# Pack output projection in 256-column strips, summed on VectorE instead of GpSimd

## The chip, the cores and the metric

One core of a Trainium2 chip runs the whole program. The metric is device time in microseconds (us) of one launch, the median over runs. TensorE (PE, with weight loads as PEld), VectorE (DVE), ScalarE (ACT), GpSimd (POOL) and SyncE (SP, which issues DMAs) each work through a queue of their own; semaphores order them against each other.

## What is computed

```python
for s in range(64):                       # 64 segments, 32 tokens each
    h = concat([mem, x_s])                # 8 memory rows + 32 tokens, 512 wide
    q, k, v = h @ Wq, h @ Wk, h @ Wv      # 32 heads of 128
    p = softmax(mask(q @ k.T * scale))    # (40 x 40 per head)
    o = (p @ v) @ Wo                      # back to 512 wide
    mem = o[:8]; out_s = o[8:]            # memory goes to the next segment
h = x + A(layernorm(x))
out = h + gelu(layernorm(h) @ w1 + b1) @ w2 + b2
```

The memory rows of one segment are the input of the next, so the 64 segments run one after another; the MLP at the end runs over all 2,048 tokens.

## The kernel before

The first 689 us are the 64 segments, some 10.3 us each; the rest is the MLP. All weights stay in SBUF. Four segments make a block (128 tokens, tile `tb`). In each segment 32 rows are handled directly: the 8 memory rows and the first 24 tokens of the segment. The last 8 tokens of each of a block's four segments do not depend on memory in their q, k and v, so they are collected into a **pack** of 32 rows, and the packs' projections are done for a whole block at a time: K of a pack in a block's first segment, Q in the second, V in the third, and the output projection of the previous block's pack (`wo_B`, L1211) in the fourth. These pieces stand in the tables `ORDERS` as F0 and F1, and they fill TensorE while the segment's own chain is elsewhere.

The chain of a segment, in the names that the profile prints: memory and tokens `hT`; projections into `ps` (L873, and L606 where weights are kept); copies `kq` on ScalarE (L891, L892); transposes `QT` and `KALL` on VectorE (L914); scores (L1042); softmax on VectorE and ScalarE (`nmc`, `EC`, `rsc`, `PC`, `PTC`); p @ v (L1080, L1085) into `quad`; copies `OT`; output projection `wo` (L1176); transpose `TT` (L1188); and two sums (L1182) that write the memory rows of the next segment's `hT`. The scores among the 24 tokens run beside it: L1110, then `nma`, `SA`, `sma`, `rsa` on VectorE, `PA` on GpSimd (L1131), `PTA`, four copies `BD` (L1137), p @ v at L1148, one segment later.

TensorE's array is used as four column groups of 32 columns. In `wo` (`wo_units`, L1166) a pair of groups takes each half of the heads and each group of a pair takes 256 output columns, so two partial sums have to be added. In `wo_B` of this kernel each group takes a quarter of the heads and all 512 output columns; the result is transposed as a whole (`TTB`, L1219), and 14 GpSimd instructions fold the four partial sums into `opT` (L1228 to L1232). `fold` hands them out over the tails of the following segments, 3, 5 and 6 at a time. Then `nat` (L1244) transposes the block's `opT` by DMA into `oN`, adds it to `xr` (L1249), takes LayerNorm statistics (L1254, L1258; GpSimd L1259, L1260) and stores the rows.

The order on ScalarE, VectorE and GpSimd is found by a scheduler when the program is built: it goes through the operations by planned times (`PLAN`, in us from the start of the segment; kinds that are not in the table go by rank) and puts each into the first gap of its engine's line that is long enough by the durations noted in the code. TensorE's order is written out in `ORDERS`. `align` (L478) gives each segment a fixed place in TensorE's blocks of 256 instructions (`PHASE`): where a segment would start elsewhere, it puts extra weight loads (L871, at most 8 in a unit of four matmuls, the same weights again) in front of its matmuls until the place is right. `wire` (L420) decides which dependences become semaphore waits.

Of the kernel before, what the change touches and what calls it, by code (L numbers as in the profile page):

```python
# [96 lines left out]
        "KB1": (12.13, None, None, None),  # L97
        "QTB1": (None, 8.75, None, None),
        "VSB1": (None, None, 10.85, None),
        "TTB": (None, None, None, 10.96)}  # L100
HOME = {'OTB': 'act', ('SC0', 0): 'act', 'ZCm0': 'pool', 'kq1': 'act', 'SP1': 'act', 'VS1': 'act', 'VSl1': 'act', 'OTm0': 'act', 'SAp': 'dve', 'PA': 'pool', 'VSB1': 'act'}
STEP = 10.28
OPEN_BANK = dict(K0=4, K1=5, Q0=6, Q1=7, V0=5, V1=4, SC0=6, SC1=7, SA=5, WO=4)
# [15 lines left out]


class Op:
    __slots__ = ("eng", "fn", "reads", "writes", "idx", "gidx", "deps", "sig", "sigcount", "waits",
                 "tag", "pad", "held", "name", "is_dma", "dma_sem", "dur", "mode", "rank", "start", "succ", "prev", "ni", "at", "dma_count", "alts", "kind", "span")

    def __init__(self, eng, fn, reads, writes, name, dur, mode):
# [15 lines left out]
class Sched:  # L141
    def __init__(self, nc, self_sync=("act", "dve", "pool")):
        self.nc = nc
        self.rec = []
        self.last_writer = {}
        self.readers = {}
        self.self_sync = set(self_sync)
        self.pe_order = []
        self.buckets = {}
        self.tag = None  # L150
        self.dmas, self.soft = [], []

    def op(self, eng, fn, reads=(), writes=(), dur=0.2, mode=0, name=None, after=(), ni=8):
        o = Op(eng, fn, tuple(reads), tuple(writes), name, dur, mode)
        o.ni = ni
        o.tag = self.tag
        o.gidx = len(self.rec)
        deps = set()
        for k in o.reads:
            excl = isinstance(k, tuple) and k[0] == "ps"  # L160
            w = self.last_writer.get(k)
            if w is not None:
                deps.add(w)
            if excl:
                deps.update(self.readers.get(k, ()))
        for k in o.writes:
            w = self.last_writer.get(k)
            if w is not None:
                deps.add(w)
            deps.update(self.readers.get(k, ()))  # L170
        deps.update(a for a in after if a is not None)
        deps.discard(o)
        o.deps = sorted(deps, key=lambda d: d.gidx)
        for k in o.reads:
            if isinstance(k, tuple) and k[0] == "ps":
                self.last_writer[k] = o
                self.readers[k] = []
            else:
                self.readers.setdefault(k, []).append(o)
        for k in o.writes:  # L180
            self.last_writer[k] = o
            self.readers[k] = []
        self.rec.append(o)
        if eng == "pe":
            if self.tag is None:
                self.pe_order.append(o)
            else:
                self.buckets.setdefault(self.tag, []).append(o)
        return o
# [230 lines left out]
    def wire(self):  # L420
# [9 lines left out]
        for o in self.all_ops:  # L430
            E = o.eng
            cand, dwaits = {}, []
            for p in o.deps:
                if p.is_dma:
                    if p not in dma_known[E]:
                        dwaits.append(p)
                    continue
                if p.eng == E and E not in self.self_sync:
                    continue
                if p.idx > cand.get(p.eng, -1):  # L440
                    cand[p.eng] = p.idx
            waits = []
            for F, i in cand.items():
                if know[E][F] >= i:
                    continue
                p = self.streams[F][i]
                p.sig = True
                waits.append(p)
            for p in waits:
                for g in engs:  # L450
                    know[E][g] = max(know[E][g], snap[p][g])
                know[E][p.eng] = max(know[E][p.eng], p.idx)
                dma_known[E] |= dsnap[p]
            for p in dwaits:
                if p in dma_known[E]:
                    continue
                waits.append(p)
                dma_known[E].add(p)
                for g in engs:
                    know[E][g] = max(know[E][g], snap[p][g])  # L460
                dma_known[E] |= dsnap[p]
            o.waits = sorted(waits, key=lambda p: -(p.start + p.dur + self.lat(p, o))) if SORT else waits
            s = dict(know[E])
            if not o.is_dma:
                s[E] = o.idx
            snap[o] = s
            ds = set(dma_known[E])
            if o.is_dma:
                ds.add(o)
            dsnap[o] = ds  # L470
# [90 lines left out]
P = 128  # L561
# [62 lines left out]
def build_kernel(nc, A_x, A_mem0, A_Wq, A_Wk, A_Wv, A_Wo, B_w1, B_b1, B_w2, B_b2, out):  # L624
# [3 lines left out]
    with st:  # L628
        def sb(name, shape, dt=BF16):
            return st.enter_context(nc.sbuf_tensor(name, shape, dt))  # L630
# [44 lines left out]
        OT = sb("OT", [P, 2, H, 32])  # L675
        OTB = sb("OTB", [P, 2, H, 32])
        TT = sb("TT", [P, 2, DC, 2, 32], F32)
        TTB = sb("TTB", [P, DC, 4, 32], F32)
        TTS = sb("TTS", [64, 2, 4, 32], F32)
        opT = sb("opT", [P, 2, DC, P])  # L680
        stt = sb("stt", [P, 2, 6], F32)
        agg = sb("agg", [P, 2, 2], F32)
# [475 lines left out]
        def slot(h):  # L1158
            j = (h % 16) // 4
            return 16 * (j // 2) + 8 * (h // 16) + 4 * (j % 2) + h % 4  # L1160
# [48 lines left out]
                    rows()  # L1209

        def wo_B(bk, bank):  # L1211
            for q in range(8):
                def f(e, q=q):
                    for j in range(4):
                        ins = e.matmul(ps[bank][32 * j:32 * j + 32, :], OTB[:, bk % 2, slot(8 * j + q), :], WO[:, 8 * j + q, :], start=(q == 0), stop=(q == 7),  # L1215
                                       tile_position=(0, 32 * j), skip_group_check=True)
                    return ins
                S.op("pe", f, reads=[("WO", g, a) for g in range(8) for a in range(2)] + [("OTB", bk % 2, sg) for sg in range(4)], writes=[("ps", bank)], dur=0.2135, mode=MC, ni=8)
            S.op("dve", lambda e: e.transpose(TTB[:].rearrange("p c q t -> p (c q t)"), ps[bank][:, :]), reads=[("ps", bank)], writes=["TTB"], dur=t_dve(512) + 0.02)  # L1219
            o = opT[:, bk % 2, :, :].rearrange("p c (s t) -> p c s t", s=4)[:, :, :, NA:SEG]  # L1220

            def chunk(c):
                t = TTB[:, c:c + 2]

                def sums(q):
                    def f(e):
                        x, y = [v[0:32, :, q].rearrange("p c (s t) -> p c s t", s=4) for v in (t, TTS)]
                        return e.tensor_tensor(o[32 * q:32 * q + 32, c:c + 2], x, y, ALU.add)  # L1228
                    return lambda after: S.op("pool", f, reads=["TTB", "TTS"], writes=[("opB", bk % 2)], dur=0.31, after=after)
                return [lambda after: S.op("pool", lambda e: e.tensor_copy(TTS[0:64], t[64:128]), reads=["TTB"], writes=["TTS"], dur=0.4, after=after),  # L1230
                        lambda after: S.op("pool", lambda e: e.tensor_tensor(t[0:64], t[0:64], TTS[0:64], ALU.add), reads=["TTB", "TTS"], writes=["TTB"], dur=0.73, after=after),
                        lambda after: S.op("pool", lambda e: e.tensor_copy(TTS[0:32], t[32:64]), reads=["TTB"], writes=["TTS"], dur=0.41, after=after)] + [sums(q) for q in range(4)]  # L1232
            folds.extend(chunk(0) + chunk(2))

        folds = []

        def fold(n, after=()):
            tag, S.tag = S.tag, None
            for f in folds[:n]:
                S.narrow(f(after))  # L1240
            del folds[:n]
            S.tag = tag

        def nat(bk):  # L1244

# [149 lines left out]
        for s in range(NS):  # L1395
# [46 lines left out]
            def tail(s):  # L1442
                S.tag = (s, "SAT")
                sa_tail(s)
                n = 14 if s == NS - 1 else (3, 5, 6, 0)[s % 4] if s // 4 < NTB - 3 else (7, 7, 0, 0)[s % 4]
                moved = []
                for f in late[::-1]:
                    moved.append(f([S.last_writer[("PTC", 1)]] + [o_ for o_ in moved if o_]))
                late[:] = now
                now.clear()  # L1450
                behind = [S.last_writer[(k, 1)] for k in ("PC", "PCa")] + [o_ for o_ in moved if o_]
                if folds:
                    fold(n, behind + [S.last_writer[("BD", s % 2, j)] for j in range(4 * (s == NS - 1))])
                if turned and s % 4 == 3:
                    for f in turned:
                        f(behind)
# [139 lines left out]
        for i in range(2):  # L1596
            f = slice(i * (F // 2), (i + 1) * (F // 2))
            for c in range(DC):
# [5 lines left out]
        busy = (BANK["FB"], BANK["WO"])  # L1604
        free = [b for b in range(4, 8) if b not in busy]
        early, later = (free + sorted(set(busy)))[:2], (free + sorted(set(busy)))[2:]
        rest = {0: lambda: wo(NS, later[-1], mem=False), 2: lambda: nat(NTB - 2), 4: lambda: pv_a(NS - 1), 5: lambda: pv_a_ev(NS - 1), 7: lambda: (wo_B(NTB - 1, later[-1]), fold(14)),
                9: lambda: wo(NS + 1, later[0], mem=False), 11: lambda: nat(NTB - 1)}
        rest = dict(zip((0, 1, 3, 4, 6, 7, 9), rest.values()))
        for n, fc in enumerate(range(3, FC)):  # L1610
# [84 lines left out]
```

## Time and profile before

| | us |
|---|---|
| median of 3 runs (804.85 to 806.24) | 805.77 |
| span of the profiled execution | 804.0 |
| PE busy | 772.7 |
| DVE busy | 616.6 |
| ACT busy | 543.0 |
| POOL busy | 350.7 |
| granted TensorE clock, mean | 0.996 |

The device time of the profiled execution is not listed apart; its span is 1.8 us under the median of the runs, and what lies around the span is taken as that. Busy shares cover the whole span: a matmul's end is modelled, so a busy PE says only that matmuls were in its pipe. What the segments wait for is read from the timeline: a row gives start, length in us, engine, line, operation, out<-in, shape and count, and in brackets how long the engine was idle before it and for whom.

### The profile page before, as it was taken

The page shows a single profiled execution, that of the slowest core. Times are in us where ns is not written, and L with a number is a line of the kernel's source. Part 1 is how long each engine was busy: PE and PEld are TensorE (multiplying, and loading weights), DVE is VectorE, ACT ScalarE, POOL GpSimd, SP SyncE. Part 2 cuts the span into 40 slices and gives each one's busy share as a digit, 9 for nine tenths or more (in the row PEclk, how much of TensorE's full clock was granted, in tenths as well). Part 3 has the DMA queues.
Part 4 walks back from the last instruction along what each step waited for, and adds up shares of the span by engine and source line. Part 5 has one row for each costly group of instructions (what it writes and reads, how often), then busy time and mean ns, then how long its engine had stood idle before and what let it go on. Part 6 is the DMA issues. An engine that isn't in the chain of part 4 may idle for free.

```text
span 804.0 us, 43669 instructions
## 1 busy us (share of the span) xinstructions
PE 772.7 (96%) x19317; PEld 419.3 (52%) x18821; DVE 616.6 (77%) x1975; ACT 543.0 (68%) x1618; POOL 350.7 (44%) x886
## 2 busy tenths in 40 slices
PE   3788999999999999999999999999999999999998
PEld 1345555555555555555555555555555555544443
DVE  3267898898989898998989898989898887824211
ACT  2456777777777777777777787777777777743342
POOL 5023334545454545454545454545463535367200
PEclk9999999999999999999999999999999999999999
DMA  9960010110101010101010102020212131264200
GB/s 338 393 188 16 4 30 11 27 34 23 37 18 42 18 43 14 46 10 47 8 50 10 49 11 51 10 51 3 51 29 63 37 87 32 89 167 132 69 27 26
DMA packets 65450, 48.04 MB, mean 60 GB/s; under 512 B 29028, under 2 KB 61676, under 8 KB 65260
## 3 DMA queue, kind: packets, MB, share of 16 engines
q1 hardware_dynamic: 64928, 44.98, 18.9%
q8 instruction: 150, 2.46, 1.3%
q14 instruction: 40, 0.33, 0.1%
q10 hardware_dynamic: 332, 0.27, 0.1%
HBM read 31.08 MB, written 8.13 MB: 49 GB/s over the span
## 4 chain that ended last, share of the span: by engine, by line
PE 91%; DVE 3%; DMA 2%; SPq 2%; ACT 1%; issue 0%
PE ps L873 43%; PE ps L1176 16%; PE ps L606 7%; PE quad L1584 6%; PE ps L1577 5%; PE ps L1215 4%; PE quad L1080 3%; DMA WQ<-in_A_Wq_dram 2%; SPq L776 2%; PE ps L1110 2%; PE quad L1042 2%; PE ps L1370 2%; PE quad L1148 1%; PE quad L1085 1%; DVE PC L1067 1%; ACT kq L891 1%
## 5 line engine op out<-in xcount | busy, mean ns | idle before, releaser
L873 PE MATMUL ps<-WQ,hT 128*32 128x512 bf16 x2048 | 157.0, 382 | 3.5 <-DVE hT L1182 3.3
L1176 PE MATMUL ps<-WO,OT 128*32 128x256 bf16 x4224 | 141.5, 275 | 1.0 <-ACT OT L891 1.0
L873 PE MATMUL ps<-WV,hT 128*32 128x512 bf16 x1780 | 138.1, 379 | 0.0
L892 ACT ACTIVATE kq<-ps 128x512 bf16<-128x512 f32 x146 | 87.2, 597 | 57.5 <-PE ps L873 57.2
L1131 POOL TENSOR_TENSOR PA<-SA,rsa 128x256 bf16<-128x256 f32 x64 | 39.8, 622 | 181.4 <-DVE rsa L1124 169.6
L891 ACT CAST kq<-ps 128x512 bf16<-128x512 f32 x160 | 93.3, 583 | 29.8 <-PE ps L873 29.8
L1176 PEld LDWEIGHTS ps<-WO,OT 128*32 128x32 bf16 x4224 | 96.2, 96 | 23.6 <-ACT OT L891 4.0
L1137 POOL COPY BD<-PTA 32x192 bf16<-32x192 bf16 x256 | 95.7, 374 | 16.5 <-DVE PTA L1133 0.8
L1067 DVE SCALAR_TENSOR_TENSOR PC<-EC,rsc,even 128x128 bf16<-128x128 f32 x256 | 94.5, 370 | 6.7
L873 PE MATMUL ps<-WK,hT 128*32 128x512 bf16 x1292 | 92.3, 379 | 0.0
L873 PEld LDWEIGHTS ps<-WQ,hT 128*32 128x32 bf16 x2048 | 56.4, 96 | 63.7 <-issue 19.3
L914 DVE STREAM_TRANSPOSE KALL<-kq 128x256 f32<-128x256 f32 x160 | 70.5, 441 | 21.3 <-ACT kq L891 19.0
L891 ACT CAST VS<-ps 128x512 bf16<-128x512 f32 x189 | 83.9, 444 | 0.9
L1059 ACT ACTIVATE EC<-quad,nmc 128x64 f32<-128x64 f32 x252 | 76.8, 310 | 5.7
L606 PE MATMUL ps<-WK,hT 128*32 128x512 bf16 x756 | 74.3, 379 | 0.0
L891 ACT CAST OT<-quad 128x128 bf16<-128x128 f32 (+1 forms) x208 | 68.4, 352 | 4.9 <-PE quad L1085 0.7
L914 DVE STREAM_TRANSPOSE QT<-kq 128x256 f32<-128x256 f32 x128 | 57.0, 446 | 16.1 <-ACT kq L892 15.0
L873 PEld LDWEIGHTS ps<-WV,hT 128*32 128x32 bf16 x1780 | 49.4, 96 | 34.9 <-issue 1.0
L1580 ACT ACTIVATE WQ<-ps,b1t 128x512 bf16<-128x512 f32 x42 | 28.9, 687 | 52.0 <-PE ps L1577 52.0
L1122 ACT ACTIVATE SA<-SA 128x256 f32<-128x256 f32 x64 | 26.7, 417 | 52.2 <-DVE SA L1121 48.8
L873 PEld LDWEIGHTS ps<-WK,hT 128*32 128x32 bf16 x1292 | 35.9, 97 | 46.6 <-issue 20.2
L1228 POOL TENSOR_TENSOR opT<-TTB,TTS 32x64 bf16<-32x64 f32 x128 | 40.3, 315 | 31.7 <-DVE opT L1182 22.5
(159 smaller groups left out, 1475.9 us busy)
## 6 DMA issues: line engine op xcount, KB each, us to landing
WV<-in_A_Wv_dram SPq DMA_DIRECT2D x4, 1024.0 KB, 10.4
WK<-in_A_Wk_dram SPq DMA_DIRECT2D x4, 1024.0 KB, 18.1
WQ<-in_A_Wq_dram SPq DMA_DIRECT2D x4, 1024.0 KB, 19.4
WO<-in_A_Wo_dram SPq DMA_DIRECT2D x16, 256.0 KB, 7.7
v_last<-VSB SPq DMA_DIRECT2D x60, 64.0 KB, 3.1
VBD<-v_last SPq DMA_DIRECT2D x60, 64.0 KB, 2.9
h_mid<-xr SPq DMA_DIRECT2D x16, 128.0 KB, 1.8
WQ<-h_mid SPq DMA_DIRECT2D x4, 512.0 KB, 4.4
```

The source lines that it names most:

```text
L606: return e.add_instruction(mybir.InstMatmult(name="I-%d" % (4000000 + _kept[0]), engine=mybir.EngineType.PE, start_tensor_calc=start, stop ...
L873: ins = e.matmul(o, l, m, start=(k == 0), stop=(k == DC - 1), tile_position=(0, 32 * j), skip_group_check=True)
L891: return {"act": (lambda e: e.copy(out, src), t_act(n, ps_)), "dve": (lambda e: e.tensor_copy(out, src), 0.155 + 1.0e-3 * n * fast)}
L892: return {"act": (lambda e: e.mul(out, src, scale_), t_act(n, ps_)), "dve": (lambda e: e.tensor_scalar(out, src, scale_, None, ALU.mult), ...
L914: S.op("dve", lambda e: e.transpose(out, src), reads=[("kq", i)], writes=[key], dur=t_dve(256) + 0.02)
L1059: return e.activation(EC[:, r, sl, :], o[:, sl, :], ACTF.Exp, bias=nmc[:, r, sl:sl + 1], accum_out=smc[:, r, sl:sl + 1])
L1067: S.op("dve", lambda e, sl=sl, xc=xc: e.scalar_tensor_tensor(PC[:, r, :, :, sl], xc, rsc[:, r, sl:sl + 1], ev, ALU.mult, ALU.mult), reads= ...
L1137: S.narrow(S.op("pool", lambda e, j=j, rows=rows: e.tensor_copy(BD[rows, par, :, j, :, :], PTA[rows, :, 0:NA, :]), reads=["PTA"], writes=[ ...
L1176: ins = e.matmul(ps[bank][32 * j:32 * j + 32, 0:256], lhs(slot(h)), wo_cols(h, b), start=(k == 0), stop=(k == 15), tile_position=(0, 32 * ...
L1228: return e.tensor_tensor(o[32 * q:32 * q + 32, c:c + 2], x, y, ALU.add)
L1577: ins = e.matmul(ps[bank][:, 0:SBT], W1[:, cc, fc * P:(fc + 1) * P], hnT_of(k)[:, cc, :], start=(cc == 0), stop=(cc == DC - 1))
L1584: S.op("pe", lambda e: e.matmul(quad[:, t, :], gT_of(k, fc)[:, t * P:(t + 1) * P], W2[:, fc, :], start=(fc == 0), stop=(fc == FC - 1)), re ...
```

## The change

`wo_B` calls `wo_units`, as `wo` does: strips of 256 columns, twice as many matmuls of half the width, two partial sums instead of four. Its transpose is 128x256 instead of 128x512, and two VectorE sums of 64 partitions write `opT` at a planned time of 12.2 us (some 1.9 us into the next segment). The 14 GpSimd instructions per pack, `TTS` and `fold` are gone. In `wire`, a dependence on the same engine no longer becomes a wait if it is one of two readers of a PSUM bank, or only an order asked for by `after`; GpSimd keeps its waits.

```diff
         "TTB": (None, None, None, 10.96),
+        "opB": (None, None, None, 12.2)}
...
             if w is not None:
                 deps.add(w)
+                if not (excl and w in self.lookers.get(k, ())):
+                    hard.add(w)
...
         deps.update(a for a in after if a is not None)
         deps.discard(o)
+        o.soft = deps - hard
...
-                if p.eng == E and E not in self.self_sync:
+                if p.eng == E and (E not in self.self_sync or (p in o.soft and E != "pool")):
                     continue
...
-        TTB = sb("TTB", [P, DC, 4, 32], F32)
-        TTS = sb("TTS", [64, 2, 4, 32], F32)
+        TTB = sb("TTB", [P, DC, 2, 32], F32)
...
         def wo_B(bk, bank):
-            for q in range(8):
-                def f(e, q=q):
-                    for j in range(4):
-                        ins = e.matmul(ps[bank][32 * j:32 * j + 32, :], OTB[:, bk % 2, slot(8 * j + q), :], WO[:, 8 * j + q, :], start=(q == 0), stop=(q == 7),
-                                       tile_position=(0, 32 * j), skip_group_check=True)
-                    return ins
...
-            S.op("dve", lambda e: e.transpose(TTB[:].rearrange("p c q t -> p (c q t)"), ps[bank][:, :]), reads=[("ps", bank)], writes=["TTB"], dur=t_dve(512) + 0.02)
+            wo_units(lambda sl: OTB[:, bk % 2, sl, :], lambda r: [("OTB", bk % 2, sg) for sg in range(4)], bank)
+            S.op("dve", lambda e: e.transpose(TTB[:].rearrange("p c q t -> p (c q t)"), ps[bank][:, 0:256]), reads=[("ps", bank)], writes=["TTB"], dur=t_dve(256) + 0.02)
             o = opT[:, bk % 2, :, :].rearrange("p c (s t) -> p c s t", s=4)[:, :, :, NA:SEG]
...
+            def sums(e):
+                for q2 in range(2):
+                    x, y = [TTB[64 * a:64 * a + 64, :, q2, :].rearrange("p c (s t) -> p c s t", s=4) for a in range(2)]
+                    ins = e.tensor_tensor(o[64 * q2:64 * q2 + 64], x, y, ALU.add)
+                return ins
+            S.op("dve", sums, reads=["TTB"], writes=[("opB", bk % 2)], dur=0.58)
...
-                if folds:
-                    fold(n, behind + [S.last_writer[("BD", s % 2, j)] for j in range(4 * (s == NS - 1))])
```

The scheduler then places other work anew. Three places matter below. The first is VectorE's queue at the start of a block's first segment (segment 24 here, counted from 0), where the pack of the segment before is transposed; line numbers of the changed kernel are about ten higher. Before:

```order
L1121 TENSOR_TENSOR SA<-ps5,nma 128x256
L1219 STREAM_TRANSPOSE TTB<-ps4 128x512
L1123 TENSOR_REDUCE sma<-SA 128x8
L1124 RECIPROCAL rsa<-sma 128x8
L914 STREAM_TRANSPOSE QT<-kq 128x256
L914 STREAM_TRANSPOSE KALL<-kq 128x256
```

The same place in the changed kernel:

```order
L1131 TENSOR_TENSOR SA<-ps5,nma 128x256
L1223 STREAM_TRANSPOSE TTB<-ps4 128x256
L1133 TENSOR_REDUCE sma<-SA 128x8
L1134 RECIPROCAL rsa<-sma 128x8
L1229 TENSOR_TENSOR opT<-TTB 64x16x8 x2
L924 STREAM_TRANSPOSE QT<-kq 128x256
L924 STREAM_TRANSPOSE KALL<-kq 128x256
```

The transpose is half as wide, and the two sums (64 partitions, 128 elements each) stand between `rsa` and the segment's first `QT`. They wait for no semaphore. This is so in 14 segments: 8, 12, and so on to 60.

The second place is VectorE's queue at the end of the same segment, where the next memory rows are made. Before:

```order
L1069 STREAM_TRANSPOSE PTC<-PC 128x128
L1182 TENSOR_TENSOR opT<-TT 64x4x24 x2
L891 CAST OT<-quad 128x16x24
L1254 BN_STATS st2<-xr 128x6
L1258 BN_AGGR agg2<-st2 128x2
L1188 STREAM_TRANSPOSE TT<-ps7 128x256
L1182 TENSOR_TENSOR hT<-TT 64x4x8 x2
```

In the changed kernel:

```order
L1079 STREAM_TRANSPOSE PTC<-PC 128x128
L1192 TENSOR_TENSOR opT<-TT 64x4x24 x2
L901 CAST OT<-quad 128x16x24
L1238 TENSOR_TENSOR xr<-xr,oN 128x512
L1243 BN_STATS st2<-xr 128x6 x2
L1198 STREAM_TRANSPOSE TT<-ps7 128x256
L1247 BN_AGGR agg2<-st2 128x2
L1192 TENSOR_TENSOR hT<-TT 64x4x8 x2
```

`opT` of the block is complete three segments earlier than with the folding, so `nat`'s DMA and its sum into `xr` (before: in the block's fourth segment) move here, with the first half of the statistics; and `agg2` now stands between `TT` and the sums into `hT`. This is so in ten segments, 12 to 48; in 8 and 56 only `xr` and one BN_STATS come in, in 52 `xr` alone, and in 60 again both.

The third place is TensorE's queue at the end of a block's fourth segment and the head of the next one. Before:

```order
L1110 MATMUL ps<-KALL,QT 32x32 x32
L1215 MATMUL ps<-WO,OTB 32x512 x12
L871 LDWEIGHTS hT
L873 MATMUL ps<-WQ,hT 32x512
L871 LDWEIGHTS hT
```

In the changed kernel:

```order
L1120 MATMUL ps<-KALL,QT 32x32 x32
L1186 MATMUL ps<-WO,OTB 32x256 x24
L881 LDWEIGHTS hT x2
L883 MATMUL ps<-WQ,hT 32x512
L881 LDWEIGHTS hT x2
```

A pack now has 64 instructions more, which moves the next segment's place in its 256-instruction block; `align` makes up the other 192 with extra weight loads, 195 instead of 3 in each of 13 segments (8, 12, to 56), eight to a unit in the first 24 units. In all there are 2,960 such loads instead of 528.

In the block's fourth segment `opT<-TT`, `xr` and `st2` leave VectorE's queue between `OT` and `TT`; `opT<-TT` now stands between `SA` and `sma`, and `xn` behind `rsa`.

More of the change, by code (lines that the diff above doesn't have):

```diff
@@ L99 @@
         "VSB1": (None, None, 10.85, None),
-        "TTB": (None, None, None, 10.96)}
+        "TTB": (None, None, None, 10.96),
+        "opB": (None, None, None, 12.2)}
 HOME = {'OTB': 'act', ('SC0', 0): 'act', 'ZCm0': 'pool', 'kq1': 'act', 'SP1': 'act', 'VS1': 'act', 'VSl1': 'act', 'OTm0': 'act', 'SAp': 'dve', 'PA': 'pool', 'VSB1': 'act'}
@@ L121 @@
 class Op:
-    __slots__ = ("eng", "fn", "reads", "writes", "idx", "gidx", "deps", "sig", "sigcount", "waits",
+    __slots__ = ("soft", "eng", "fn", "reads", "writes", "idx", "gidx", "deps", "sig", "sigcount", "waits",
                  "tag", "pad", "held", "name", "is_dma", "dma_sem", "dur", "mode", "rank", "start", "succ", "prev", "ni", "at", "dma_count", "alts", "kind", "span")
@@ L146, in __init__ @@
         self.readers = {}
+        self.lookers = {}
         self.self_sync = set(self_sync)
@@ L157, in op @@
         o.gidx = len(self.rec)
-        deps = set()
+        deps, hard = set(), set()
         for k in o.reads:
@@ L169, in op @@
                 deps.add(w)
+                hard.add(w)
             deps.update(self.readers.get(k, ()))
+            hard.update(self.readers.get(k, ()))
         deps.update(a for a in after if a is not None)
         deps.discard(o)
+        o.soft = deps - hard
+        for k in o.reads:
+            self.lookers.setdefault(k, set()).add(o)
+        for k in o.writes:
+            self.lookers[k] = set()
         o.deps = sorted(deps, key=lambda d: d.gidx)
@@ L1211, in wo_B @@
         def wo_B(bk, bank):
-            for q in range(8):
-                def f(e, q=q):
-                    for j in range(4):
-                        ins = e.matmul(ps[bank][32 * j:32 * j + 32, :], OTB[:, bk % 2, slot(8 * j + q), :], WO[:, 8 * j + q, :], start=(q == 0), stop=(q == 7),
-                                       tile_position=(0, 32 * j), skip_group_check=True)
-                    return ins
-                S.op("pe", f, reads=[("WO", g, a) for g in range(8) for a in range(2)] + [("OTB", bk % 2, sg) for sg in range(4)], writes=[("ps", bank)], dur=0.2135, mode=MC, ni=8)
@@ L1219, in wo_B @@
-            S.op("dve", lambda e: e.transpose(TTB[:].rearrange("p c q t -> p (c q t)"), ps[bank][:, :]), reads=[("ps", bank)], writes=["TTB"], dur=t_dve(512) + 0.02)
-            o = opT[:, bk % 2, :, :].rearrange("p c (s t) -> p c s t", s=4)[:, :, :, NA:SEG]
[L1222 to L1242, printed above, removed]
+            wo_units(lambda sl: OTB[:, bk % 2, sl, :], lambda r: [("OTB", bk % 2, sg) for sg in range(4)], bank)
+            S.op("dve", lambda e: e.transpose(TTB[:].rearrange("p c q t -> p (c q t)"), ps[bank][:, 0:256]), reads=[("ps", bank)], writes=["TTB"], dur=t_dve(256) + 0.02)
@@ L1444, in tail @@
                 sa_tail(s)
-                n = 14 if s == NS - 1 else (3, 5, 6, 0)[s % 4] if s // 4 < NTB - 3 else (7, 7, 0, 0)[s % 4]
                 moved = []
@@ L1606, in build_kernel @@
         early, later = (free + sorted(set(busy)))[:2], (free + sorted(set(busy)))[2:]
-        rest = {0: lambda: wo(NS, later[-1], mem=False), 2: lambda: nat(NTB - 2), 4: lambda: pv_a(NS - 1), 5: lambda: pv_a_ev(NS - 1), 7: lambda: (wo_B(NTB - 1, later[-1]), fold(14)),
+        rest = {0: lambda: wo(NS, later[-1], mem=False), 2: lambda: nat(NTB - 2), 4: lambda: pv_a(NS - 1), 5: lambda: pv_a_ev(NS - 1), 7: lambda: wo_B(NTB - 1, later[-1]),
                 9: lambda: wo(NS + 1, later[0], mem=False), 11: lambda: nat(NTB - 1)}
```

## The prediction

> **What bounds the kernel.** I read the chain of work that ended last first: it is TensorE for nine tenths.
>
> ```profile
> PE 91%; DVE 3%; DMA 2%; SPq 2%; ACT 1%; issue 0%
> 289.04 1.73 PE ps L873 x30
> 299.26 1.73 PE ps L873 x32
> 309.60 1.73 PE ps L873 x24
> ```
>
> But the three rows below the shares, from the chain in order of time (start, length), stand at one and the same place of segments 24, 25 and 26, and are 10.22 and 10.34 us apart, though the work on TensorE is the same to a few hundredths. So I asked who waits, TensorE's weight loads first.
>
> ```profile
> PEld quad L1080 <- DVE rsc L1064: 32.2, 64, 1.1
> PEld L871 <- DVE hT L1182: 21.1, 48, 1.3
> PEld quad L1042 <- DVE KALL L914: 13.1, 62, 0.2
> ```
>
> Every segment's scores wait for VectorE's `KALL` (62 of 64), p @ v waits for VectorE's softmax (64 of 64), and a segment's first loads wait for the sums into `hT`. The filler on TensorE hides most of each wait, and the segments are still one chain through VectorE: `hT`, projections, `QT`, `KALL`, scores, softmax, p @ v, `wo`, `TT`, `hT`. **What delays VectorE at one of these places delays everything behind it.** So GpSimd's 44% and VectorE's 77% say little; the order on VectorE at these places says nearly all.
>
> **Front of a block's first segment.** Segment 24 of before, VectorE:
>
> ```profile
> 288.75 0.71 DVE L1219 STREAM_TRANSPOSE TTB<-ps 128x512 f32<-128x512 f32 x1
> 289.38 0.38 DVE L1123 TENSOR_REDUCE sma<-SA 128x8 f32<-128x256 f32 x1
> 289.79 0.20 DVE L1124 RECIPROCAL rsa<-sma 128x8 f32<-128x8 f32 x1
> 290.36 0.45 DVE L914 STREAM_TRANSPOSE QT<-kq 128x256 f32<-128x256 f32 x1 [0.37 <-ACT kq L892]
> 290.84 0.45 DVE L914 STREAM_TRANSPOSE KALL<-kq 128x256 f32<-128x256 f32 x1
> 295.44 0.52 DVE L1182 TENSOR_TENSOR opT<-TT 64x96 bf16<-64x96 f32 x2
> 295.99 0.56 DVE L891 CAST OT<-quad 128x384 bf16<-128x384 f32 x1
> 297.75 0.39 DVE L1182 TENSOR_TENSOR hT<-TT 64x32 bf16<-64x32 f32 x2
> 288.87 0.42 ACT L1122 ACTIVATE SA<-SA 128x256 f32<-128x256 f32 x1 [2.52 <-DVE SA L1121]
> ```
>
> The new `TTB` has the shape of `TT` (0.45, its row is below) instead of 0.71. `sma` starts 0.08 ahead of `TTB`'s end (289.46), so an overlap of that much is allowed; with the shorter `TTB` it waits for ScalarE's exponential (ends 289.29): a gain of about 0.06. `rsa` ends at 289.93. Behind it come the two new sums. A pair of 32 elements takes 0.39, one of 96 takes 0.52, 0.065 per 32; a pair of 128 alone would take 0.59. It would end at 290.55 and move `QT` by 0.2 and `KALL`, which stands 0.03 behind `QT`'s end and can overlap it by that 0.08, by 0.13.
>
> But it is not alone. `rsa` also releases `PA` on GpSimd. Before, such a pair stands behind `rsa` just once, in the last segment:
>
> ```profile
> 701.10 0.20 DVE L1124 RECIPROCAL rsa<-sma 128x8 f32<-128x8 f32 x1
> 701.34 0.85 DVE L1182 TENSOR_TENSOR opT<-TT 64x96 bf16<-64x96 f32 x2
> 701.39 0.69 POOL L1131 TENSOR_TENSOR PA<-SA,rsa 128x256 bf16<-128x256 f32 x1 [5.88 <-DVE rsa L1124]
> L1131 POOL TENSOR_TENSOR PA<-SA,rsa x64: 617/619/688, 51.9 to 701.4; 128x256 bf16<-128x256 f32 x64
> ```
>
> The pair took 0.85 instead of 0.52, and `PA` 0.69 instead of its median 0.62 (its group of 64, the last row): the first sum held `PA` up, `PA` held up the second sum, which ended 0.11 behind `PA`. The new sums have the same form, two float32 tiles in SBUF on 64 partitions. By this row: `PA` starts at 290.02, ends 0.69 and another 0.03 later (the first sum is a third longer) at 290.74; the second sum ends 0.14 behind it at 290.88; `QT` starts at 290.90 instead of 290.36, `KALL` at 290.90 + 0.45 - 0.08 = 291.27 instead of 290.84. The segment's scores wait for that `KALL`, nothing ahead of p @ v catches up, since `nmc` and the softmax follow the scores on VectorE. I take **0.45** per segment, from this single case, the nearest row; the ends are 0.13 (no collision) and 0.6. 14 segments: **6.3 us** (1.8 to 8.4).
>
> **Back of the same segment.** The order that the change makes here, `xr`, two statistics, `TT`, `agg`, `hT`, stands in before in segments 58 and 62; 58 is:
>
> ```profile
> 645.37 0.53 DVE L891 CAST OT<-quad 128x384 bf16<-128x384 f32 x1
> 645.83 0.41 DVE L1249 TENSOR_TENSOR xr<-xr,oN 128x512 bf16<-128x512 bf16 x1
> 646.27 0.75 DVE L1254 BATCH_NORM_STATS2 st<-xr 128x6 f32<-128x256 bf16 x2
> 647.00 0.45 DVE L1188 STREAM_TRANSPOSE TT<-ps 128x256 f32<-128x256 f32 x1
> 647.38 0.17 DVE L1258 BATCH_NORM_AGGREGATE agg<-st 128x2 f32<-128x12 f32 x1
> 647.57 0.39 DVE L1182 TENSOR_TENSOR hT<-TT 64x32 bf16<-64x32 f32 x2
> ```
>
> From the end of `OT` (645.90) to that of `hT` (647.96) it is 2.06. In the changed kernel the first statistics do not read this `xr`, so they need not wait for it (0.11 less), and `TT` does not wait for TensorE (0.07 less): 1.88. In segment 24 `OT` ends at 296.55, or 0.03 earlier without the GpSimd copy beside it; `hT` would end at 298.40 instead of 298.14. Both ends shift with the front alike, so it adds: **0.26** in ten segments, **2.6 us** (bounds 0.1 to 0.4 each). In segments 8 and 56 `TT` is still later than what is put ahead of it; 52 costs 0.1. `oN`'s landing does not decide: issued once the sums end (2.9 us into the segment), it lands 2.5 us after (4.2 at most), and `xr` starts at 8.5.
>
> ```profile
> DMA to landing us min/median/max: 2.4/2.5/4.2
> ```
>
> **What is gained.** GpSimd's copies collide with the sums into `hT` the same way. In a block's second segment:
>
> ```profile
> 307.83 0.39 POOL L1230 COPY TTS<-TTB 64x256 f32<-64x256 f32 x1
> 308.00 0.48 DVE L1182 TENSOR_TENSOR hT<-TT 64x32 bf16<-64x32 f32 x2
> L1182 DVE TENSOR_TENSOR hT<-TT 64x32 bf16<-64x32 f32 x126 | 25.1, 199 | 3.0
> ```
>
> 0.48 instead of 0.39; and the group of all 126 sums has 25.1 us, where 126 of 0.188 (0.39 for two, less the 0.014 between) would be 23.7. All of it is on the chain and due to the folds: **-1.4 us**. In the fourth segments VectorE is rid of this, here of segment 27:
>
> ```profile
> 326.66 0.79 DVE L1182 TENSOR_TENSOR opT<-TT 64x96 bf16<-64x96 f32 x2
> ...
> 328.27 0.43 DVE L1188 STREAM_TRANSPOSE TT<-ps 128x256 f32<-128x256 f32 x1
> ```
>
> There `TT` was late by 0.14, because `opT` met another GpSimd copy (0.79 instead of 0.52); that happened in four segments (11, 27, 35, 43; 0.07 to 0.17): **-0.5 us**. Elsewhere TensorE sets `TT`. The moves of `agg` in the last blocks cancel (out of 58 and 62, into 57).
>
> **TensorE.** The strips cost nearly nothing; the same 32 rows by both forms, from the chain:
>
> ```profile
> 708.54 1.84 PE ps L1215 x32
> 711.35 1.86 PE ps L1176 x64
> ```
>
> 0.02 a pack, 0.3 for 16, hidden under the waits in the segments except for the last two packs, 0.04; with the 0.1 of segment 52 I take 0.1. The extra loads: segment 4 of before has 67, eight in each of its first units, segment 8 only 3 (first unit of the segment, and its scores).
>
> ```profile
> 82.58 0.41 PE L873 MATMUL ps<-WQ,hT 128*32 128x512 bf16 x4 [0.77 <-DVE hT L1182]
> 83.46 0.13 PEld L871 LDWEIGHTS <-hT 128*32 128x32 bf16 x8
> 86.04 0.30 PE L1042 MATMUL quad<-KALL,ZC 128*32 128x64 bf16 x16
> 123.57 0.40 PE L873 MATMUL ps<-WQ,hT 128*32 128x512 bf16 x4
> 127.03 0.29 PE L1042 MATMUL quad<-KALL,ZC 128*32 128x64 bf16 x16
> ```
>
> 3.46 us from the first to the other in both: the loads run under the matmuls. Only the eight ahead of a segment's first matmul, which wait for the same `hT` as it does, have nothing to run under: at most 13 x 0.13 = 1.7 (the row of eight loads); I take 0, since by the rows above segment 4 has its scores no later behind its first matmul than segment 8. [...]
>
> **Waits left out.** They are ScalarE's second reads of a bank (`VS`, `OTB`) and VectorE orders such as `opT` behind `PTC`. In the queues other work mostly stands between the two:
>
> ```profile
> L891 ACT CAST OTB<-quad 128x256 bf16<-128x256 f32 x64 | 24.0, 375 | 0.1
> ```
>
> 0.1 us idle ahead of 64 of them: nothing to gain; bounds 0 to -0.1 there, and VectorE's orders are in the back's sum.
>
> **Sum.** 6.3 + 2.6 + 0.1 - 1.4 - 0.5 = +7.1 us on the profiled span, 804.0 to 811.1. The runs' median lies 1.8 above that span, so **805.77 + 7.1 = 812.9 us**.
>
> **Rivals.** (1) The pair does not meet `PA`: if both sums are through before `PA` starts, the front costs 0.13 and not 0.45, and the sum is 1.8 + 2.6 + 0.1 - 1.9 = +2.6: 808.4. Against it: `PA` starts 0.09 behind `rsa` in the row above, while one sum takes 0.29. Chance 0.14. (2) Faster: if the scores had 0.45 of slack behind `KALL`, and `TT` 0.26 ahead of the next `hT`, only the relief of GpSimd would be left, -1.9 + 0.1: 804.0. It decides at the wait for `KALL`; its 13.1 us in 62 waits say that the loads are already waiting there, 0.2 each. Chance 0.05. (3) The padded loads are not hidden where they run on into V and the scores: at 0.13 for eight (row above), 24 units, 13 segments, up to 41 us, 854 with the rest. Chance 0.03. (4) The front is longer than the single case: `PC` meets the `BD` copies, which both move, or the 13 more instruction blocks that the loads make collide with `oN`; 0.2 more per first segment, 815.7. Chance 0.08. The forecast has 0.70.
>
> A change within 0.2%, 1.6 us, could not be told from none. Slower by more: forecast, (3), (4) and most of (1), 0.90. Within: the rest of (1), part of (2): 0.06. Faster: 0.04. The range takes in (1) and the bounds of the front: 807.8 to 815.5.
>
> **What would show it.** Right: in the changed profile the pair `opT<-TTB` takes some 0.9 instead of 0.59 and `PA` beside it 0.7; the first segments' `QT` comes 0.5 later; first segments grow from 10.22 to 10.9, second ones shrink from 10.33 to 10.24, third ones stay. Wrong: a pair of 0.59; first segments of 10.5 or less; gaps between matmuls of padded units over 0.22; a `TT` that still waits for TensorE in the first segments.

## Result and the profile after

| | before | after |
|---|---|---|
| median of 5 runs, us | 805.77 (804.85 to 806.81) | 833.95 (830.73 to 834.81) |
| ratio, 95% interval | | 1.034 (1.032 to 1.036) |
| span of the profiled execution, us | 804.0 | 832.6 |
| PE, DVE, ACT busy, us | 772.7, 616.6, 543.0 | 782.6, 621.3, 542.9 |
| POOL busy, us | 350.7 | 261.4 |
| segments by place in their block, median of 12, us | 10.22, 10.33, 10.22, 10.28 | 12.08, 10.50, 10.22, 10.28 |

The change costs 28.2 us; the forecast had 7.1. A segment's length is the time from one end of the sums into `hT` to the next, in segments 8 to 55. First segments are 1.9 us longer, not 0.7. Line numbers of after are some ten higher than before's. One of the 12 executions of run 14 below, at 1,290 us with a granted clock of 0.56, is left out of its ratio.

The chain's shares on the page of after, and the chain's rows that answer to those of segments 24 to 26 (start, length):

```profile
PE 90%; issue 3%; DMA 2%; DVE 2%; SPq 2%; ACT 1%
298.26 1.73 PE ps L883 x32
310.43 1.73 PE ps L883 x32
320.68 1.73 PE ps L883 x24
```

They stand 12.17 and 10.25 us apart, and 3% of the chain (before 0%) is issue, time in which TensorE waited for nothing that the profile shows. The view of waits says where (us in total, times, longest), TensorE's matmuls first, then three rows of its loads that answer to before's:

```profile
PE ps L883 <- issue: 10.4, 13, 1.3
PE ps L1120 <- issue: 7.8, 17, 0.9
PEld quad L1090 <- DVE rsc L1074: 23.8, 53, 0.9
PEld L881 <- DVE hT L1192: 14.4, 34, 1.3
PEld quad L1052 <- DVE KALL L924: 12.8, 56, 0.5
```

The waits for VectorE became shorter. In the same view of before no matmul waits for issue. Segment 24 of after, TensorE's rows with such a wait:

```profile
296.51 0.22 PE L1120 MATMUL ps<-KALL,QT 128*32 128x32 bf16 x7 [0.61 <-issue]
299.80 0.82 PE L617 MATMUL ps<-WK,hT 128*32 128x512 bf16 x4
304.51 0.39 PE L883 MATMUL ps<-WV,hT 128*32 128x512 bf16 x1 [0.86 <-issue]
308.61 0.30 PE L1120 MATMUL ps<-KALL,QT 128*32 128x32 bf16 x20 [0.28 <-issue]
```

The second row hides one: four matmuls that take 0.40 elsewhere take 0.82, with the hole inside. Now count instructions from one hole's end to the next. The view of stretches gives the length and each engine's busy time with (x) its instructions, PE and PEld being the first two, and the granted clock behind the fifth:

```profile
296.50:300.24 3.74, 3.69 (x82) 2.50 (x174) 3.18 (x9) 1.68 (x4) 0.72 (x1) 1.00 0.02 4
300.24:304.49 4.25, 3.40 (x84) 2.62 (x170) 3.60 (x15) 2.88 (x11) 2.35 (x7) 1.00 0.17 35
304.49:308.60 4.11, 3.82 (x125) 2.62 (x126) 3.08 (x10) 2.81 (x10) 0.00 (x0) 1.00 0.02 4
```

82 + 174 = 256, 84 + 170 = 254, 125 + 126 = 251. The view leaves out semaphore waits; the trace has 0, 2 and 5 of them here, which makes 256 each time. **TensorE stops here after each 256 instructions**, whatever they are, and goes on 3.7 to 4.3 us after it last did. The whole trace agrees: between 60 and 720 us, in 152 blocks of 256, there are 37 holes of over 0.25 us that wait for issue, all at one and the same place of the 256, and where two follow each other directly (19 times) they are 3.7 to 4.4 us apart. The clock is 1.00 throughout. The transfers of this stretch, in 40 slices of 0.31 us (GB/s), and the DMA queue that the page calls instruction:

```profile
GB/s 0 0 0 53 0 0 0 0 0 0 0 0 0 0 10 203 198 15 53 0 0 0 0 0 0 0 0 0 0 0 0 53 0 0 0 0 0 0 0 0
q8 instruction: 164, 2.69, 1.4%
```

Each 53 is one packet of 16 KB (2.69 MB / 164), begun at 297.6, 302.2 and 306.0. 1.4% of 16 engines over 832.6 us is 1.1 us a packet. By the times of the single packets, a hole ends 1.2 to 1.6 us after a packet is in, and the next packet begins 1 to 2 us after a hole's end (all 37). Before, this queue had 150 packets. The trace of before has 38,557 records of TensorE with the semaphore waits, 150.6 blocks of 256; that of after has 42,004, 164.1 blocks. So about one packet goes with each block, and every hole ends at nearly the same time behind one: the packets are read here as TensorE's instructions. In the trace of before, blocks begin 3.70 us apart or more (60 to 720 us), and no matmul waits for issue.

What the forecast said of VectorE and GpSimd did happen, under these holes. The pair and `PA` in segment 24, then the segment's back:

```profile
298.61 0.20 DVE L1134 RECIPROCAL rsa<-sma 128x8 f32<-128x8 f32 x1
298.84 0.92 DVE L1229 TENSOR_TENSOR opT<-TTB 64x128 bf16<-64x128 f32 x2
298.89 0.72 POOL L1141 TENSOR_TENSOR PA<-SA,rsa 128x256 bf16<-128x256 f32 x1 [4.79 <-DVE rsa L1134]
306.09 0.41 DVE L1238 TENSOR_TENSOR xr<-xr,oN 128x512 bf16<-128x512 bf16 x1
306.42 0.75 DVE L1243 BATCH_NORM_STATS2 st<-xr 128x6 f32<-128x256 bf16 x2
308.10 0.45 DVE L1198 STREAM_TRANSPOSE TT<-ps 128x256 f32<-128x256 f32 x1 [0.93 <-PE ps L1186]
L1192 DVE TENSOR_TENSOR hT<-TT 64x32 bf16<-64x32 f32 x126 | 23.7, 188 | 3.0
```

The pair takes 0.92 beside a `PA` of 0.72 (forecast 0.9 and 0.7). So do all 15 pairs that meet `PA` (0.91 to 0.92, `PA` 0.72); the one that meets none, at 739.5 us, takes 0.59. `TT` waits 0.93 for TensorE (0.39 to 1.13 in 13 of the 14 first segments), so the back's order costs nothing here. The last row is the group of all sums into `hT`: 23.7 us, as forecast, from 25.1.

### The profile page after: what moved, and what is told of

Read it like the earlier page. It is cut to its first block, busy times and chain, and to the rows that moved or that the text cites. A ratio compares the mean times of both kernels' runs of the same rounds, so it can differ in the third digit from the quotient of the medians.

```text
span 832.6 us, 46858 instructions
## 1 busy us (share of the span) xinstructions
PE 782.6 (94%) x19820; PEld 452.7 (54%) x21765; DVE 621.3 (75%) x2007; ACT 542.9 (65%) x1618; POOL 261.4 (31%) x662
## 3 DMA queue, kind: packets, MB, share of 16 engines
q8 instruction: 164, 2.69, 1.4%
## 4 chain that ended last, share of the span: by engine, by line
PE 90%; issue 3%; DMA 2%; DVE 2%; SPq 2%; ACT 1%
PE ps L883 42%; PE ps L1186 19%; PE ps L617 7%; PE quad L1570 6%; PE ps L1563 4%; PE quad L1090 3%; PE ps L1120 2%; DMA WQ<-in_A_Wq_dram 2%; SPq L786 2%; PE quad L1052 2%; PE ps L1359 2%; PE quad L1158 1%; PE quad L1095 1%; DVE PC L1077 1%; ACT kq L901 0%
## 5 line engine op out<-in xcount | busy, mean ns | idle before, releaser
L883 PE MATMUL ps<-WV,hT 128*32 128x512 bf16 x1780 | 144.9, 380 | 10.4 <-issue 10.4
L1141 POOL TENSOR_TENSOR PA<-SA,rsa 128x256 bf16<-128x256 f32 x64 | 41.9, 654 | 274.3 <-DVE rsa L1134 261.9
L1147 POOL COPY BD<-PTA 32x192 bf16<-32x192 bf16 x256 | 94.0, 367 | 16.3 <-DVE PTA L1143 0.6
L883 PE MATMUL ps<-WK,hT 128*32 128x512 bf16 x1292 | 94.3, 379 | 0.0
L617 PE MATMUL ps<-WK,hT 128*32 128x512 bf16 x756 | 77.8, 379 | 0.3
L883 PEld LDWEIGHTS ps<-WV,hT 128*32 128x32 bf16 x1780 | 54.4, 96 | 42.2 <-issue 18.0
L881 PEld LDWEIGHTS <-hT 128*32 128x32 bf16 x2752 | 50.5, 96 | 32.6 <-DVE hT L1192 14.4
L1198 DVE STREAM_TRANSPOSE TT<-ps 128x256 f32<-128x256 f32 x66 | 29.6, 449 | 48.5 <-PE ps L1186 47.4
```

Of the source, the lines that this page charges most:

```text
L617: return e.add_instruction(mybir.InstMatmult(name="I-%d" % (4000000 + _kept[0]), engine=mybir.EngineType.PE, start_tensor_calc=start, stop ...
L881: e.ldweights(l, tile_position=(0, 32 * j))
L883: ins = e.matmul(o, l, m, start=(k == 0), stop=(k == DC - 1), tile_position=(0, 32 * j), skip_group_check=True)
L1141: S.either({k: ((lambda e: e.tensor_tensor(PA[:].rearrange("p a t b -> p a b t"), SA[:].rearrange("p (a b) t -> p a b t", b=2), bc2, ALU.m ...
L1147: S.narrow(S.op("pool", lambda e, j=j, rows=rows: e.tensor_copy(BD[rows, par, :, j, :, :], PTA[rows, :, 0:NA, :]), reads=["PTA"], writes=[ ...
```

## Experiments

Two theories stood at first. **Fetch theory**: TensorE runs out of instructions where a block of 256 is used up faster than the next arrives. **Load theory**: each extra load costs TensorE time of its own (rival 3 of the prediction). The forecast's VectorE order and the transposing DMA of `oN`, which now runs in the first segment next to a fetch, were rivals for part of it. Times are medians; "before" is that of the same chip, 805.9 to 806.2. Segments are given by place in the block, in us, as in the table above.

**1. Extra loads spread.**

```diff
-PHASE = (0, 64, 128, 192)
-LATE = {60: 60}
+PHASE = (192, 80, 192, 64)
+LATE = {}
```

> The changed kernel with another PHASE (192, 80, 192, 64) and no LATE: the extra loads are spread over the four segments of a block (0, 80, 51 and 66 instead of 195, 0, 3 and 2), 3,600 in all instead of 2,960, so that TensorE's instruction blocks begin at least 3.55 us apart by the planned times, instead of 3.0. Fetch theory (TensorE runs out of fetched instructions where a block of 256 is used up faster than the next arrives): the waits put down to issue ahead of V and the scores among tokens go, first segments come to 10.9 us, what is left is the forecast of VectorE's order, 809 to 814 us. Load theory (each extra load takes TensorE time of its own, 28.2 us / 2,432 extra loads = 11.6 ns): 640 more loads, 833.9 + 7 = 841 us.

818.0 us, ratio 1.015 (1.013 to 1.017). Segments 11.03, 10.24, 10.23, 10.34. With 640 loads more than after it is 16 us faster: load theory is out. The waits for issue ahead of V and of the scores are gone; second segments are at the 10.24 that was forecast. It is 4 us above the expected range: first segments are 0.81 longer than before's, not 0.7, and the fourth did not shrink.

**2. `oN` late.**

```diff
-reads=[("opA", bk % 2, k) for k in range(4)] + [("opB", bk % 2)], writes=["oN"])
+reads=[("opA", bk % 2, k) for k in range(4)] + [("opB", bk % 2)], writes=["oN"], after=[S.last_writer[("hTm", s % RING)]])
```

> The changed kernel, extra loads as they are; only the transposing DMA of oN waits for the sums that start a block's fourth segment, as late as before the change, and xr and its statistics go back there with it. Fetch theory with the DMA in it (the fetch begun in the first segment stands behind oN's packets): first segments lose 0.6 to 1.1 us of their 12.1, and 0.26 behind OT, 14 of them: 815 to 825 us. Fetch theory without it, and load theory: only the 0.26 behind OT, 830 to 832 us.

831.9 us, ratio 1.032 (1.030 to 1.034): at most the small share, as the interval overlaps that of after. `oN`'s DMA beside the fetch is not the cause: without it packets still begin 1.1 to 2.1 us after a hole's end.

**3. Both.**

> Both edits together. By the terms of the prediction the back of the first segments (2.6 us) goes and the front (6.3) stays: 805.8 + 6.3 + 0.1 - 1.4 - 0.5 = 810.3 us, 1.5 to 3.5 us below the run with the spread loads alone. If the front's 0.45 is hidden, 804 us. Load theory: 838 us.

817.0 us, ratio 1.0135 (1.012 to 1.015), 7 above the expectation. Segments 10.78, 10.41, 10.23, 10.38. First segments fall by 0.26, exactly the back's term; second and fourth ones rise by 0.17 and 0.04, so that only 1 us is left of it. The rise of the second segments is at their head, here that of segment 25:

```profile
300.64 0.39 DVE L1192 TENSOR_TENSOR hT<-TT 64x32 bf16<-64x32 f32 x2
301.25 0.13 PEld L881 LDWEIGHTS <-hT 128*32 128x32 bf16 x8 [0.50 <-DVE hT L1192]
```

The sums into `hT` end at 301.03, and the first load, which stands at the edge of a block of 256, starts 0.22 later; in this run's other segments, whose heads lie elsewhere in a block, it is 0.05. It is 0.17 to 0.39 in all 12 second segments, and 0.05 in 10 of the 12 of run 1, whose heads have the same place. The packet had been in for 1.5 to 2.0 us by then. Whether the load waits for its block or for the step into it was not tested.

Segment 24 starts at 290.26 here, VectorE:

```profile
292.11 0.20 DVE L1134 RECIPROCAL rsa<-sma 128x8 f32<-128x8 f32 x1
292.34 0.92 DVE L1229 TENSOR_TENSOR opT<-TTB 64x128 bf16<-64x128 f32 x2
293.27 0.45 DVE L924 STREAM_TRANSPOSE QT<-kq 128x256 f32<-128x256 f32 x1
293.64 0.40 DVE L924 STREAM_TRANSPOSE KALL<-kq 128x256 f32<-128x256 f32 x1
296.20 0.49 DVE L1077 SCALAR_TENSOR_TENSOR PC<-EC,rsc,even 128x128 bf16<-128x128 f32 x1
```

`QT` starts 3.01 us into the segment (before 2.44), `KALL` ends at 3.78 (before 3.37). A `PC` of 0.49, where its place has 0.36 before, now stands beside the `BD` copies (rival 4), and the segment is 0.55 longer.

**4. The kernel before with as many TensorE instructions.**

```diff
                     for j in range(4):
+                        for _ in range(2):
+                            e.ldweights(OTB[:, bk % 2, slot(8 * j + q), :], tile_position=(0, 32 * j))
                         ins = e.matmul(ps[bank][32 * j:32 * j + 32, :], ...
-S.op("pe", f, ..., dur=0.2135, mode=MC, ni=8)
+S.op("pe", f, ..., dur=0.2135, mode=MC, ni=16)
```

> The kernel before, with 8 loads of the same weights more in front of each unit of wo_B (64 per pack, written over by the loads that follow), nothing else: as in the change, align answers with 195 extra loads in first segments. Strips, VectorE sums, waits and the place of oN are those of before. Fetch theory: the stalls come back without the change, less those that oN's DMA makes: 815 to 828 us. Load theory: 2,432 + 960 loads, 834 us or more. Theory that VectorE's order is the cause: 806 us.

832.5 us, ratio 1.032 (1.030 to 1.034); segments 12.03, 10.41, 10.22, 10.31. Its waits:

```profile
PE ps L873 <- issue: 7.7, 12, 1.2
PE ps L1110 <- issue: 7.5, 19, 0.8
```

**No strip, no VectorE sum, no wait left out, and 26.3 of the 28.2 us are there.** The other 1.9 are not clear of the noise. All 40 holes of its trace stand at one place of the 256, too. The expected upper end (828) was too low; `oN` had been given a share that run 2 takes from it.

**5. The pair away from `rsa`.** Run 3 with the sums put behind `opA` of the same segment.

```diff
-        "opB": (None, None, None, 12.2)}
+        "opB": (8.2, None, None, None)}
...
+                while parked and s % 4 == 0:
+                    moved.append(parked.pop()([S.last_writer[("PTC", 1)]] + [S.last_writer[("OTx", s % 2, t)] for t in range(2)] + [o_ for o_ in moved if o_]))
```

> Run 3 (spread loads, late oN) with the two new sums taken away from behind rsa and put behind opA at 7.9 us of the same segment, ahead of the statistics; one OT copy goes to ScalarE for it. If the pair behind rsa is what makes first segments longer (10.77 against 10.22 us, 0.55 in each of 14): they come to 10.25 to 10.35, 809 to 811 us. If something else of the change does (the transpose, a wait left out, what is left of fetch stalls): 816 to 817 us as in run 3.

810.4 us, ratio 1.006 (1.0045 to 1.007). First segments are at 10.26. Second ones are at 10.53: their heads, at the edge of a block again, start 0.13 to 0.36 behind `hT`. In segment 24, which starts at 288.33:

```profile
290.78 0.45 DVE L924 STREAM_TRANSPOSE QT<-kq 128x256 f32<-128x256 f32 x1 [0.39 <-ACT kq L902]
296.39 0.59 DVE L1229 TENSOR_TENSOR opT<-TTB 64x128 bf16<-64x128 f32 x2
```

Away from `PA` the pair takes 0.59, the length that the prediction gave it without a collision, and `QT` is back at 2.45. The front is worth 6.6 us (817.0 - 810.4; 6.3 if each run is taken against its own chip's before).

**6. No extra loads.** Run 5 with `PHASE = ()`.

> Run 5 without any extra loads (PHASE empty, so align adds none): 2,368 instead of 2,560 TensorE instructions per four segments, blocks 4.4 us apart in the mean, but at changing places; at 17 of them the plan has 3.0 to 3.5 us between two. Fetch theory: at most 0.5 us at each of those, 805 to 812 us, below run 5. Load theory: 3,600 loads fewer than run 5, 42 us less than it, about 770 us.

808.6 us, ratio 1.0035 (1.002 to 1.005). With 3,600 loads fewer it is 1.8 us faster, where load theory had 42. The 1.8 are not the price of the loads alone, as both runs lose time at blocks: run 5 in its second segments, this one in single segments of 10.6 to 11.6. The medians are 10.25, 10.21, 10.20 and 10.35.

**7. The kernel before with 64 loads more in each segment.**

```diff
-PHASE = (0, 64, 128, 192)
-LATE = {60: 60}
+PHASE = (0, 128, 0, 128)
+LATE = {}
```

> The kernel before with PHASE (0, 128, 0, 128) and no LATE: 64 extra loads in every segment, 4,560 in all instead of 528, ten blocks of instructions in four segments as after the change, but at least 3.4 us apart by the plan. Fetch theory: little is lost, 806 to 813 us. Load theory at 11.6 ns for each of 4,032 loads: 852 us.

813.9 us, ratio 1.009 (1.008 to 1.011), where load theory had 852. It is just above the fetch range: blocks 3.4 us apart by the plan are already a little too close (segments 10.42, 10.51, 10.24, 10.33).

**8. Only the waits.** The kernel before with the edits in `wire` and `op` alone.

```diff
-                if p.eng == E and E not in self.self_sync:
+                if p.eng == E and (E not in self.self_sync or (p in o.soft and E != "pool")):
```

> The kernel before with nothing but the waits between two readers of a PSUM bank, and of mere orders, left out. The prediction has 0 to -0.1 us: 805.5 to 806.5. If those waits cost their 0.04 us or more at 160 places: 800 to 803 us.

806.2 us, ratio 1.0005 (0.9995 to 1.0016): nothing, as forecast. The 0.04 us in the expectation is what the kernel's own plan takes for such a wait (`HOP`); at 160 places it would be 6.4 us, and this run shows none of it.

**9 and 10. Few loads, placed for the fetches.** Run 6 with a target for every segment in `LATE`.

> Run 6 (strips, VectorE sums behind opA, late oN) with 1,222 extra loads, put where no two blocks of instructions begin less than 3.54 us apart by the plan (a target for each segment in LATE). In the traces so far a starved TensorE gets a new block every 3.8 to 4.2 us; with 4.0 us and a sequencer 0.6 us ahead nothing waits here. Fetch theory: run 6 loses its long segments (some 4 to 5 us in all), 802.5 to 805 us, faster than before. If the gains of the change are not real: 806 us or more.

> As run 9, with 1,198 loads placed for blocks at least 3.41 us apart, many of them between 3.41 and 3.5. Fetch theory: equal to run 9 if 4.0 us hold, up to 4 us more if single fetches take longer: 802.5 to 809 us.

The 0.6 us ahead, here and in run 11, is an estimate. The packets bear it out: in before the next begins 0.80 us after a block's first instruction (median of 141 between 60 and 700 us, nine tenths of them 0.16 to 1.26), in the changed kernel 1.46 us after a hole's end (median of 37). By the difference the sequencer is some 0.66 us further ahead of the array where nothing waits.

808.2 us, ratio 1.003 (1.002 to 1.004), and 809.8 us, ratio 1.005 (1.003 to 1.007). Run 9 missed its range, run 10 by 0.8 us. In run 9 first segments have 10.24, but 13, 21, 29, 37, 45 and 53 have 10.46 to 10.62, with their head at the edge of a block (0.25 to 0.35 behind `hT`), and six fourth segments have 10.4 to 11.1. In one of the two longest, 23, VectorE's row is

```profile
286.67 0.52 DVE L1192 TENSOR_TENSOR opT<-TT 64x96 bf16<-64x96 f32 x2 [0.85 <-DMA oN<-opT]
```

a wait of run 2's own making: `oN`, issued late, still reads the buffer into which `opT` writes.

**11. The 195 loads elsewhere.** Run 4 with `PHASE = (0, 64, 64, 128)`.

> Run 4 (the kernel before with 64 loads more per pack) with the 195 extra loads in the third segments instead of the first, where no transfer runs and neither oN nor the pack's sums are. Blocks then begin 3.05, 3.4 and 3.04 us apart at three places. Fetch theory with 4.0 us per block and 0.6 us ahead: 25 us (10 at 3.8, 43 at 4.2), so 816 to 835 us, the waits at the second scores and the third segments' end. If it needs the first segment's transfers or VectorE work: 806 to 808 us.

825.5 us, ratio 1.025 (1.023 to 1.028); segments 10.88, 10.36, 10.89, 10.50. The stalls move to where the blocks are close: second scores of third segments and the front of first ones.

```profile
PE ps L873 <- issue: 4.1, 10, 0.7
PE quad L1042 <- issue: 2.5, 7, 0.6
```

Third segments hold no transfers but those of instructions (segments 22, 26, 30 and 34), so the stalls need no other.

**12. Loads saved.** Run 6 with 542 extra loads, placed by `PHASE` and `LATE`, and with another order of the projections, in all four tables, the first of them shown:

```diff
-('Q0', 2, 3), ('Q1', 0, 1), ('Q0', 3, 4), ('K0', 2, 4), ('Q1', 1, 4), ('K1', 0, 4),
+('Q0', 2, 3), ('K0', 2, 3), ('Q0', 3, 4), ('K0', 3, 4), ('Q1', 0, 4), ('K1', 0, 4),
...
-('V0', 1, 4), ('F1', 0, 1), ('SC1', 0, 99), ('V1', 1, 2), ('F1', 1, 2), ('V1', 2, 4),
+('V0', 1, 2), ('V1', 1, 2), ('V0', 2, 4), ('SC1', 0, 99), ('F1', 0, 1), ('V1', 2, 4), ('F1', 1, 2),
```

> Run 6 (strips, VectorE sums behind opA, late oN) with the projections of a segment taken in another order, so that more matmuls find their weights still in the array (K0's third and fourth unit straight behind Q0's, V1's second behind V0's): the 64 instructions that the strips add per block of segments are saved elsewhere, nine blocks of instructions in four segments as before the change, at least 3.48 us apart by the plan, with 542 extra loads in all. Fetch theory: no segment is long any more, and first, second and fourth segments have the 10.24, 10.21 and 10.27 us of run 6's undisturbed ones: 801 to 804 us, faster than before. If fewer instructions don't help, or the new order costs on TensorE's chain: 807 us or more.

813.6 us, ratio 1.010 (1.008 to 1.012): missed. Hardly any fetch stall is left (1.3 us in three waits for issue), but the copies fell into another order. Fourth segments have 10.48, since `wo`'s loads wait for a copy of `OT` that ScalarE now does behind two mask copies:

```profile
371.52 0.56 PEld L1186 LDWEIGHTS ps<-WO,OT 128*32 128x32 bf16 x24 [0.34 <-ACT OT L901]
```

**13 and 14. `oN` a segment earlier**, without and with K0's kept weights. Both are run 9 with `oN`'s DMA moved; run 14 has other targets in `LATE` as well, and the copies `kq0` on ScalarE.

```diff
-... after=[S.last_writer[("hTm", s % RING)]])
+... after=[S.last_writer[("hTm", (s - 1) % RING)]])
```

> Run 9 with oN's DMA issued from the start of the third segment instead of the fourth; xr keeps its place in the fourth. If what run 9 lost in fourth segments (10.4 to 11.1 us in 23, 27, 31, 43, 47 and 55, where VectorE's opT waited up to 0.85 us for oN, which reads the same opT buffer) is oN's landing: those come to 10.3, 3 to 4 us in all, 803.5 to 806 us. If it is stalls in fetching: 807 to 809 us as in run 9.

> Run 13 with K0's last two units straight behind Q0's, so that their weights are kept (14 instructions fewer in each segment, 2,312 instead of 2,368 per block before the extra loads), V's order as before; 1,318 extra loads placed anew. Fetch theory: the second segments that run 9 had at 10.55 (13, 21, 29, 37, 45, 53) go back to 10.24, 2 us: 801.5 to 804 us. If K0's earlier place costs on ScalarE or VectorE, as the other order did in run 12: 806 us or more.

807.5 us, ratio 1.002 (1.001 to 1.003), and 808.2 us, ratio 1.0025 (1.001 to 1.004). In run 13 fourth segments come to 10.30 and the longest are 10.6, so `oN`'s landing was a part of run 9's loss; the time gains only 0.7 us of the 3 to 4 expected. In run 14 undisturbed segments have 10.24, 10.21, 10.19 and 10.26, three of them shorter than before's, but twelve second, third and fourth ones have 10.4 to 10.6. No version beats the kernel before. Six of the eleven long segments of run 13, and eight of these twelve, have their head within four instructions of a block's edge and start 0.14 to 0.34 behind `hT`. What makes the others long was not settled.

## Why the prediction was wrong

**The step that failed is "The extra loads"**, set at 0 in "TensorE". It compared segment 4 of before (67 extra loads) with segment 8 (3), saw 3.46 us in both, and concluded that loads run under matmuls. That holds: run 1 with 640 loads more is 16 us faster. But a load is also an instruction, and the comparison asked only what it costs in the array. 64 more instructions per pack and 192 more in front of a first segment make ten blocks of 256 out of nine per 41 us, and by the plan set three of them 3.0 to 3.5 us apart, where a starved TensorE gets one in 3.7 to 4.4. By run 4 that is **26.3 us**, where the sum had 0. Run 4 has none of the terms that the forecast did count, and is not clearly faster than the changed kernel: under the holes they hardly show. No matmul waits for issue in before, whose closest blocks are 3.7 us apart by the plan and by the trace, so its trace shows no price; the front of this document says that `align` gives each segment a place in blocks of 256, and that was the sign to ask why.

**Rival 3** named the place (V and the scores) and a size of up to 41 us, for a wrong reason and at 0.03: it let the loads take time. Runs 1, 6 and 7 exclude that. Rival 4's second half (more instruction blocks that collide with `oN`) was nearer, but run 2 takes `oN` out of it. Two of the prediction's signs of being wrong were there: a unit with extra loads with a hole between its matmuls, and a `TT` that waits for TensorE in first segments.

**Front: right.** Pair 0.92, `PA` 0.72; the term was 6.3 us, and run 5 against run 3 gives 6.3 to 6.6. Per segment it is 0.42 at `KALL`, as worked out (0.43), and 0.55 at the end, most likely because of the `PC` beside `BD`, which takes 0.13 longer.

**Back: right in size, not additive.** 0.26 per segment between runs 1 and 3, as forecast; the sum of times shows 1.0 of 2.6 us, because other segments lengthened, second ones at a block's edge. In the changed kernel itself `TT` waits for TensorE and the term is hidden.

**Gains: right.** The `hT` sums fall from 25.1 to 23.7 us; second segments to 10.24 in run 1; fourth segments of after have 10.285 in the mean instead of 10.326, the 0.5 us of late `TT`.

**Waits: right**, nothing (run 8). **Strips**: no cost of their own in the array was seen; their cost is the 64 instructions.

With the loads spread (run 1) the changed kernel took 818.0 us, still 5 above the forecast: first segments gain 0.81 instead of 0.71 (1.4 us in 14), fourth ones rise to 10.34 instead of falling (some 1.4), and from the last sums into `hT` to the end it is 116.4 us instead of 114.7, which the forecast had not looked at. Why the last two rise was not tested.

## What to carry to other kernels

In this case TensorE, where it waited for instructions, got 256 of them in 3.7 to 4.4 us. Where a kernel gets through 256 in less than that, count its instructions as well as its busy time. By the plan's closest two blocks, 3.7 us cost nothing here, 3.4 cost 8 us (run 7) and 3.0 cost 26 (run 4). See how many blocks the instruction queue moves, how far apart they begin, and whether a change (also padding meant to help) sets any two closer than the fetch takes. "Issue" waits at one and the same place of the 256, as the 37 of the changed kernel, point to it; adding the same number of harmless instructions to the old kernel, as in run 4, separates it from everything else the change does. And a row that shows an operation to be free in one place says so for that place only.

## What the runs showed of the hardware

- TensorE starved of instructions resumes every 256 instructions after 3.7 to 4.4 us (19 intervals in the changed kernel; from 3.5 in runs 2 and 4), though the 16 KB packet itself takes about 1.1 us.
- A segment's first load that stands at the edge of a block of 256 starts 0.13 to 0.39 us behind the sums that it waits for in all 12 second segments of runs 3 and 5, where the other segments of run 3 have 0.05.
- The two VectorE sums `opT<-TTB` over float32 tiles in SBUF take 0.91 to 0.92 us beside GpSimd's `PA`, an operation of the same kind, which then takes 0.72 instead of 0.62 (15 pairs of the changed kernel); apart from it they take 0.59 (its 16th pair, and run 5).
- Two runs that differ by 3,600 weight loads beside matmuls differ by 1.8 us (run 5 against run 6, which has none). That is 0.5 ns a load as an estimate, since both also lose time at blocks.
